# Earlier loads and earlier crossbar transposes in a windowed attention kernel with a gated feed-forward block

## The chip, the cores and the metric

One core of one Trainium2 chip. Times are device microseconds of whole executions; a profile's span is some 1.8 us shorter than the time of the same execution.

## The reference

Attention with a window of 128 and four sink tokens over 4 batches, 8 heads, 768 tokens and a head size of 64, then a gated feed-forward block on the 3072 tokens (512 to 1536 to 512):

```python
keep   = (pos_k < 4) | ((0 <= pos_q - pos_k) & (pos_q - pos_k < 128))
scores = np.where(keep, q @ k.T / 8, -1e9)
x      = softmax(scores) @ v                 # -> [3072, 512]
g      = x @ w_gate
out    = (g / (1 + np.exp(-g)) * (x @ w_val)) @ w_out
```

## The kernel before

Tokens go in twelve groups of 256. Scores of the first three groups read keys and queries transposed by TensorE; from group 3 on the sync queue transposes them on the way from SBUF to SBUF, through the crossbar, which is what `C(g)` does. The feed-forward work is a list of units, gate units and down units, over token tiles of 256, 256, 256, 512 and more. Attention steps hang on these units by number ("slots"), so that TensorE has matmuls to do meanwhile. VectorE works its own instructions in the order in which the program wrote them. A step may append work for VectorE to `later`; `flush()` at the end of a unit writes it out.

```python
def cross_T(g):
    t = crossp.tile([P, 2, 2, NP2, P], BF16, tag="kqT", name="kqT")
    for j in range(2):
        nc.sync.dma_start(t[:, j]..., nat[g][:, j]..., transpose=True)
    cross[g] = t

def step_ks(b):                    # sink keys and values of batch b
    ...
        nc.vector.tensor_copy(out=dst[r, :, h * NS:(h + 1) * NS],
            in_=... else cross[b * GC][r, 0, 0, :, 0:NS])
    nc.vector.tensor_tensor(vsb, vcf[...], diag_h[...], op=ALU.mult)

def gate(tb, f, attn):
    pg = project(wgs, "pg")        # TensorE into one PSUM bank
    th = ...                       # tanh on ScalarE
    for a in attn: a()             # the attention steps of this slot
    pv = project(wvs, "pv")
    # VectorE: u = (th + 1) * pg ; ht = u * pv
    flush()

def C(g):
    def last():
        cross_T(g)
        if g % GC == 0:            # groups 3, 6, 9: first of a batch
            later.append(A(step_ks, g // GC))
        next_load(g)
    return [last]
```

TensorE writes its products to PSUM, a memory of which this kernel takes a pool of eight banks, used in turn. When the turn comes round to a bank that VectorE has not read yet, TensorE stops.

The softmax here doesn't subtract the row's maximum and nothing guards it: scores larger than these inputs give would overflow.

## Time and profile before

| | before |
|---|---|
| time, median of 4 runs (lowest to highest) | 250.97 us (250.53 to 251.37) |
| span of the profiled run | 251.8 us |
| TensorE busy | 236.2 us |
| group 3's scores begin, after a wait of | 58.60 us, 1.58 us |
| VectorE waits for crossbar transposes | none |

The profiled run of this kernel took 253.56 us as timed. The lines of its profile are in the prediction. Two more matter for what came: the small sink copy of group 3 on VectorE, and the four crossbar transposes of groups 3 and 4 on the sync queue. In the timeline, a line is start, duration, engine, source line, operation and operands, and in brackets how long the engine was idle before it and for what.

```profile
46.32 12.80 SPq L285 DMA_TRANSPOSE kqT<-kq  x4
55.59 0.34 DVE L295 COPY ks<-kqT 64x16 bf16<-64x16 bf16 x2
```

The copy reads what the first of these transposes writes. It has no bracket: when VectorE came to it, the data were there.

### The profile page before, as it was taken

To read this page: it belongs to the slowest core of one execution; us is meant where nothing else is said; L and a number is where in the kernel's file an instruction comes from. 1 tells how busy PE (TensorE), PEld (TensorE's weight loads), DVE (VectorE), ACT (ScalarE), POOL (GpSimd) and SP (SyncE) were. 2 spreads that over 40 slices of the span, in tenths; PEclk is the share of its full clock that TensorE was granted. 3 is DMA by queue.
4 is the path that set the end of the run, shared out by engine and by line. 5 is a ranking of instruction groups with operands and counts; after the bars stand their busy time and mean duration, and the time that the engine had idled before them with its cause. 6 is when DMAs were issued, how large, how long until landed. Compare 5 with 4: busy or idle time off the path is not lost.

```text
span 251.8 us, 5130 instructions
## 1 busy us (share of the span) xinstructions
PE 236.2 (94%) x2043; PEld 133.8 (53%) x2043; DVE 161.7 (64%) x339; ACT 110.7 (44%) x219; POOL 67.6 (27%) x89
## 2 busy tenths in 40 slices
PE   7887889997999969999999999999999999999993
PEld 3456677885645424545345455445454445478441
DVE  3566878987753439995089894098991289887100
ACT  2646548336281346451283741374721562333121
POOL 4956446764595049203400000000000000000000
PEclk9999999999999979999999999999999999999999
DMA  6999999999999999936990162800263200200132
GB/s 160 127 192 186 205 189 196 158 124 146 128 179 202 230 170 136 96 44 141 177 185 0 22 108 65 205 24 1 41 86 104 107 0 0 44 0 0 53 116 85
DMA packets 102808, 27.90 MB, mean 111 GB/s; under 512 B 89984, under 2 KB 99712, under 8 KB 102784
## 3 DMA queue, kind: packets, MB, share of 16 engines
q0 software_dynamic: 71392, 13.64, 67.5%
q1 hardware_dynamic: 30816, 13.41, 25.1%
q10 hardware_dynamic: 576, 0.52, 0.8%
q8 instruction: 16, 0.26, 0.4%
q14 instruction: 8, 0.07, 0.1%
HBM read 28.34 MB, written 6.29 MB: 138 GB/s over the span
## 4 chain that ended last, share of the span: by engine, by line
PE 67%; DMA 20%; DVE 4%; POOL 4%; issue 2%; ACT 1%; SPq 1%; DVEq 0%; ACTq 0%
PE pd L462 25%; PE pv L434 18%; PE pg L434 16%; DMA kq<-in_q_dram 9%; DMA kqT<-kq 6%; DMA wg<-in_moe_w_gate_dram 4%; PE o L370 4%; PE s L323 3%; DVE u L447 1%; DMA st<-in_q_dram 1%; DVE ht L448 1%; DVE e L335 1%; POOL kq L96 1%; POOL va L123 1%; POOL kq L107 1%
## 5 line engine op out<-in xcount | busy, mean ns | idle before, releaser
L434 PE MATMUL pv<-xT,wv 128*128 128x256 bf16 (+1 forms) x384 | 75.1, 329 | 1.8 <-DMA wv<-in_moe_w_val_dram 1.1
L434 PE MATMUL pg<-xT,wg 128*128 128x256 bf16 (+1 forms) x384 | 74.6, 327 | 1.4 <-DMA wg<-in_moe_w_gate_dram 0.7
L441 ACT ACTIVATE th<-pg 128x512 f32<-128x512 f32 x72 | 43.4, 606 | 68.8 <-PE pg L434 68.3
L447 DVE SCALAR_TENSOR_TENSOR u<-th,pg 128x512 bf16<-128x512 f32 x72 | 49.2, 683 | 31.3 <-ACT th L441 30.9
L462 PE MATMUL pd<-wo,ht 128*128 128x512 bf16 x288 | 66.3, 379 | 0.0
L448 DVE TENSOR_TENSOR ht<-u,pv 128x512 bf16<-128x512 bf16 x72 | 49.5, 688 | 14.3 <-PE pv L434 7.3
L434 PEld LDWEIGHTS <-wg 128*128 128x128 bf16 x384 | 37.4, 98 | 28.3 <-issue 2.5
L330 ACT ACTIVATE e<-s 128x512 bf16<-128x512 f32 (+1 forms) x96 | 46.0, 582 | 6.2 <-PE s L323 6.1
L434 PEld LDWEIGHTS <-wv 128*128 128x128 bf16 x384 | 34.7, 98 | 22.4 <-issue 3.2
L462 PEld LDWEIGHTS <-ht 128*128 128x128 bf16 x288 | 26.8, 98 | 29.0 <-issue 0.3
L466 ACT ACTIVATE ot<-pd 128x512 f32<-128x512 f32 x24 | 14.5, 603 | 53.7 <-PE pd L462 53.7
L335 DVE TENSOR_TENSOR e<-e,mask 128x1024 bf16<-128x1024 bf16 (+1 forms) x48 | 29.3, 642 | 5.3 <-ACT e L330 5.2
L107 POOL DMA_DIRECT2D kq<-in_k_dram x18 | 16.0, 889 | 30.6 <-DMA kqT<-kq 26.8
L123 POOL DMA_DIRECT2D va<-in_v_dram x24 | 21.4, 901 | 10.1 <-DMA kq<-in_q_dram 3.8
L370 PEld LDWEIGHTS <-e 128*128 128x128 bf16 x352 | 16.6, 98 | 7.7 <-DVE e L335 1.9
L382 DVE TENSOR_TENSOR xn<-o,rcp 128x256 bf16<-128x256 f32 x46 | 19.5, 424 | 1.6
L370 PE MATMUL o<-va,e 128*128 128x65 bf16 x352 | 18.4, 193 | 1.2 <-DVE e L335 1.1
L107 POOL DMA_DIRECT2D kq<-in_q_dram x18 | 16.1, 892 | 3.0 <-DMA kq<-in_q_dram 1.5
L323 PE MATMUL s<-kqT 64*128 64x256 bf16 (+1 forms) x192 | 11.0, 243 | 3.5 <-DMA kqT<-kq 3.5
L375 DVE RECIPROCAL rcp<-o 128x4 f32<-128x4 f32 x48 | 8.3, 176 | 8.6 <-PE o L370 8.6
L323 PEld LDWEIGHTS <-kqT 64*128 64x128 bf16 x192 | 6.4, 96 | 10.1 <-issue 8.0
L370 PE MATMUL o<-vsb,es 128*128 128x260 bf16 x32 | 8.8, 275 | 0.4 <-ACT es L350 0.4
(55 smaller groups left out, 79.5 us busy)
## 6 DMA issues: line engine op xcount, KB each, us to landing
out_dram<-ot SPq DMA_DIRECT2D x24, 256.0 KB
va<-in_v_dram POOLq DMA_DIRECT2D x24, 128.0 KB, 8.6
kq<-in_k_dram POOLq DMA_DIRECT2D x18, 128.0 KB, 8.3
kq<-in_q_dram POOLq DMA_DIRECT2D x18, 128.0 KB, 8.1
wo<-in_moe_w_out_dram POOLq DMA_DIRECT2D x4, 384.0 KB, 12.4
wg<-in_moe_w_gate_dram POOLq DMA_DIRECT2D x4, 256.0 KB, 8.6
wv<-in_moe_w_val_dram POOLq DMA_DIRECT2D x4, 256.0 KB, 8.9
st<-in_q_dram ACTq DMA_DIRECT2D x4, 128.0 KB
```

The costliest lines, as they stand in the source:

```text
L107: nc.gpsimd.dma_start(x[:, j, i].rearrange("p (h d) -> p h d", d=D), src[b, :, t0:t0 + P].rearrange("h m d -> m h d"))
L123: nc.gpsimd.dma_start(va[:, j, :, 0:D], v[b, :, t0:t0 + P].rearrange("h m d -> m h d"))
L323: nc.tensor.matmul(pss[2 * pp + h][:, col:col + n * P], keys(b, t, r, p), queries(g, r, p, j, n), start=True, stop=True)
L330: nc.scalar.activation(e_t[g][:, h0 + h, lo:512], pss[2 * pp + h][:, lo:512], AF.Exp, scale=scale)
L335: nc.vector.tensor_tensor(e, e, m[:, :, lo:512].broadcast_to([P, 2, 512 - lo]), op=ALU.mult)
L370: nc.tensor.matmul(o, l, r, start=(i == 0), stop=(i == len(mms) - 1), skip_group_check=True)
L382: nc.vector.tensor_tensor(xns[g, j][:, 256 * hh:256 * (hh + 1)].rearrange("p (h d) -> p h d", h=4), po[:, :, 0:D], rcp.broadcast_to([P, 4, ...
L434: nc.tensor.matmul(ps[:, i * n:(i + 1) * n], ws[fi][:, c, fo * P:(fo + 1) * P], x[:, 0:n // P, c], start=(c == 0), stop=(c == DMC - 1))
L441: nc.scalar.activation(th, pg, AF.Tanh, scale=0.5)
L447: nc.vector.scalar_tensor_tensor(u, th, 1.0, pg, op0=ALU.add, op1=ALU.mult)
L448: nc.vector.tensor_tensor(hts[tb][:, f:f + two].rearrange("p a n -> p (a n)"), u, pv, op=ALU.mult)
L462: nc.tensor.matmul(po, hts[tb][:, f, ts * P:(ts + 1) * P], wos[f // n][:, f % n], start=(f == 0), stop=(f == DFC - 1))
```

## The change

The intent: bring data sooner (two larger loads per queue for the first group, GpSimd's loads no longer held back, the second group ahead of the second weight pair), and issue each crossbar transpose early, so that it only waits for its own data. The schedule of attention steps moves along, and one down unit goes in among the gate units.

```diff
-    for p in range(NP2):
-        st = opool.tile([P, 2, 4 * D], FP32, tag="ot", name="st")
+    for k2 in range(2):
+        st = natp.tile([P, 4, 4 * D], FP32, tag="kq", name="st")
...
-    give = const.tile([P, 1], FP32)
-    nc.gpsimd.tensor_copy(out=give, in_=first[0][:, 0, 0:1])
     load_v(0); load_gate(0)
+    load4(1)
     load_gate(1)
-    load4(1)
...  (first group: tile 1 is normalised first, on ScalarE)
-    us = [g0[0], g0[1], (alone, 0, 0), *g0[2:5], *g1, g0[5], *g2,
-          *downs(0), *downs(1), *downs(2)]
+    us = [g0[0], (alone, 0, 0), *g0[1:4], *g1, *g0[4:6], downs(0)[0], *g2,
+          downs(0)[1], *downs(1), *downs(2)]
...
-        (14, C(3)), ((16, 17), Ss(3)), (17, C(4)), ((18, 18, 19, 19), PVs(3)),
+        ... (10, K(2)), (10, C(3)), ... (13, C(4)),
+        ((16, 17), Ss(3)), ((18, 18, 19, 19), PVs(3)),
...
+        (22, C(5)), ((22, 22, 23, 23), PVs(4)), (24, Xs(4))))
     weave(gates(3) + downs(3), slots(
-        (0, C(5)), *pair(5, 6, 2), (3, C(6)), (12, C(7))))
+        *pair(5, 6, 2), (2, C(6)), (10, C(7))))
```

(One-line forms above are shortened from the source; slots of groups 1 and 2 are left out.)

More of the change, by code (lines that the diff above doesn't have):

```diff
@@ L167 @@
     first = []
-    for p in range(NP2):
-        st = opool.tile([P, 2, 4 * D], FP32, tag="ot", name="st")
+    for k2 in range(2):
+        st = natp.tile([P, 4, 4 * D], FP32, tag="kq", name="st")
         for i, src, eng in ((0, k, nc.sync), (1, q, nc.scalar)):
             eng.dma_start(st[64 * i:64 * (i + 1)],
-                          four_tokens(src, 0, slice(2 * p, 2 * p + 2)))
+                          four_tokens(src, 0, slice(4 * k2, 4 * k2 + 4)))
         first.append(st)
@@ L208 @@
     nc.vector.tensor_copy(out=flat0[:, 3 * P:4 * P], in_=flat[:, 3 * P:4 * P])
-    give = const.tile([P, 1], FP32)
-    nc.gpsimd.tensor_copy(out=give, in_=first[0][:, 0, 0:1])
     load_v(0)
     load_gate(0)
+    load4(1)
     load_gate(1)
-    load4(1)
-    load_gate(2)
     load_v(1)
-    load_gate(3)
-    load_gate(4)
+    for i in range(2, 5):
+        load_gate(i)
     kTs, qTs, es_t, e_t, xns, xTs = {}, {}, {}, {}, {}, {}
@@ L541 @@
     for ph in range(2):
-        transpose(0, ph, lambda p: first[p], id32)
+        transpose(0, ph, lambda p: first[ph][:, 2 * p - 4 * ph:2 * p - 4 * ph + 2], id32)
     step_S(0, 0)
@@ L546 @@
     warm(3)
+    pro(*[lambda: None] * 3)
+    step_PV(0, 1, 0, True)
+    step_PV(0, 0, 0)
+    later.insert(0, later.pop(1))
     flush()
-    for hh in range(2):
-        pro(A(step_PV, 0, 0, hh), A(step_PV, 0, 1, hh, True))
-        flush()
+    step_PV(0, 1, 1, True)
+    step_PV(0, 0, 1)
+    flush()
     warm(2)
@@ L565 @@
     g0, g1, g2 = gates(0), gates(1), gates(2)
-    us = [g0[0], g0[1], (alone, 0, 0), *g0[2:5], *g1, g0[5], *g2,
-          *downs(0), *downs(1), *downs(2)]
+    us = [g0[0], (alone, 0, 0), *g0[1:4], *g1, *g0[4:6], downs(0)[0], *g2,
+          downs(0)[1], *downs(1), *downs(2)]
     weave(us, slots(
-        (1, T(1)), (2, Ss(1) + [K(1)]), (4, PVs(1) + [flush]),
-        (5, [A(step_X, 1, 0), A(step_X, 1, 1, True), flush]),
-        (7, T(2)), ((8, 9), Ss(2)), (9, [K(2)]),
-        (10, PVs(2)[:2] + [flush]), (11, PVs(2)[2:] + [flush]),
-        (12, [A(step_X, 2, 0), A(step_X, 2, 1, True), flush]),
-        (14, C(3)), ((16, 17), Ss(3)), (17, C(4)), ((18, 18, 19, 19), PVs(3)),
+        (0, T(1)), (1, Ss(1) + [K(1)]), (3, PVs(1) + [flush]),
+        (4, [A(step_X, 1, 0), A(step_X, 1, 1, True), flush]),
+        (8, T(2)), ((9, 10), Ss(2)), (10, [K(2)]), (10, C(3)),
+        (11, PVs(2)[:2] + [flush]), (12, PVs(2)[2:] + [flush]),
+        (13, [A(step_X, 2, 0), A(step_X, 2, 1, True), flush]), (13, C(4)),
+        ((16, 17), Ss(3)), ((18, 18, 19, 19), PVs(3)),
         (20, Xs(3)), ((20, 21), Ss(4)), (21, [K(4)]),
-        ((22, 22, 23, 23), PVs(4)), (24, Xs(4))))
+        (22, C(5)), ((22, 22, 23, 23), PVs(4)), (24, Xs(4))))
     def pair(ga, gb, sh=0):
@@ L585 @@
     weave(gates(3) + downs(3), slots(
-        (0, C(5)),
-        *pair(5, 6, 2), (3, C(6)), (12, C(7))))
+        *pair(5, 6, 2), (2, C(6)), (10, C(7))))
     weave(gates(4) + downs(4), slots(*pair(7, 8), (3, C(8)), (10, C(9)), (14, C(10))))
```

## The prediction

> **What bounds the kernel now.** I read the page first, then the chain of work that ended last in order of time, then the waits of TensorE with its timeline, then the table of stretches around the two longest waits. The page says where the time can be.
>
> ```profile
> PE 236.2 (94%) x2043; PEld 133.8 (53%) x2043; DVE 161.7 (64%) x339; ACT 110.7 (44%) x219; POOL 67.6 (27%) x89
> PEclk9999999999999979999999999999999999999999
> DMA  6999999999999999936990162800263200200132
> ```
>
> TensorE is busy 236.2 of 251.8 us, so no schedule without less work gains more than 15.6 us, and part of that is the ends (1.43 us before the first matmul, some 3.5 us of last eviction and store). The DMA row is full for the first seventeen slices of 6.3 us: until about 107 us the loads are limited by supply. The clock row has one dip, in slice 15 (88.1 to 94.4 us). The chain shows which waits count:
>
> ```profile
> 0.81 3.07 DMA st<-in_q_dram
> 3.96 0.55 DMA vcf<-in_v_dram
> 5.07 1.93 POOL va L123 x2
> ...
> 11.28 10.82 DMA wg<-in_moe_w_gate_dram
> 22.38 0.69 POOL kq L96
> 23.21 12.56 DMA kq<-in_q_dram
> ...
> 38.32 9.81 DMA kq<-in_q_dram
> 48.19 10.28 DMA kqT<-kq
> 58.60 0.51 PE s L323 x8
> ...
> 84.43 0.60 ACT ot L466
> 85.49 1.28 SPq L285
> 86.87 3.90 DMA kqT<-kq
> 90.82 0.93 PE s L323 x10
> 91.75 1.82 PE pv L434 x4
> 93.57 1.25 PE pg L434 x4
> 94.82 0.86 PE pv L434 x4
> ```
>
> Up to 58.6 us the end is set by loads alone: from the wait of GpSimd for the first queries, through its queue of loads, to the queries of group 3 at 48.13 us, and 10.28 us of crossbar transposes behind those. TensorE has other waits before that (1.12 us for the second group's queries at 20.19, 0.23, 0.52 and 1.12 us for weights at 26.02, 29.95 and 32.58), but they are not on the chain: what they cost is given back at 58.6, where TensorE sits idle anyway. The second joint is at 84.43: the sync queue issues group 5's transposes only after the last store of the third token tile, whose eviction ends at 85.03. The timeline of TensorE has the waits themselves, and the table of stretches the clock behind the second:
>
> ```profile
> 58.60 0.51 PE L323 MATMUL s<-kqT 64*128 64x256 bf16 x8 [1.58 <-DMA kqT<-kq]
> 89.80 0.23 PE L323 MATMUL s<-kqT 64*128 64x128 bf16 x2 [1.14 <-DMA kqT<-kq]
> 90.82 0.93 PE L323 MATMUL s<-kqT 64*128 64x256 bf16 x10 [0.79 <-DMA kqT<-kq]
> 91.00:92.00 1.00, 1.00 (x11) 0.51 (x8) 0.00 (x0) 0.67 (x2) 0.38 (x1) 0.50 1.01 191
> ```
>
> The seventh figure after the stretch is the granted clock: 0.50. The clock record of the trace has it at half from 90.81 to 94.23 us. So the second wait costs twice: 1.14 + 0.79 = 1.93 us idle, and then the ten score matmuls take 0.93 us where the same kind takes about 0.45, the four "pv" 1.82 where the next four take 0.86, the four "pg" 1.25 against 0.86: 0.48 + 0.96 + 0.39 = 1.83 us more.
>
> **What the Trainium skill says.** "TensorE: Matmul & The Clock Gate", Part 1: TensorE's clock is gated to half after an idle window of about 3.4 us, and the windows run freely. The trace agrees on the length (3.41 us at half) and narrows the condition: the window before the drop, 87.40 to 90.81, was 1.93 us idle (56%), while the window 56.68 to 60.09 was 1.58 us idle (46%) and nothing dropped. "DMA: Bandwidth & Descriptors", Issuing engines are not separate DMA queues: transfers from the sync, scalar and GpSimd queues run on the same 16 engines and interleave. The trace agrees: between 48.2 and 58.6 us the transposes (0.60 MB) and the GpSimd loads (0.80 MB) share 136 GB/s. The same page, Specifications: below 512 B a transfer does not run at line rate. The trace agrees: loads that write 128-byte rows run at 154 GB/s (44 to 48 us), loads that write 512-byte rows at 192 (12 to 20 us), counted in what they write.
>
> **The change part by part.**
>
> First, the first keys and queries come by two loads of 256 KB per queue in place of four of 128 KB. The bytes are the same; the packets of these two queues flow without a gap from 2.3 to 6.5 us in the trace of before, so the engines set their pace, not the four issues of 0.65 us. Saved on the path: nothing. The second half may land a little later, because GpSimd's loads now run beside it.
>
> Second, the copy "give" goes, which held GpSimd from 2.53 until the first tile had landed (4.54), so that its loads began at 5.07. They can now begin at about 3.0 to 3.5 (a memset on VectorE at 3.22 comes before the first). In before, GpSimd's first bytes flow at 6.87, 1.8 us after its first issue; from 6.5 to 7.2 the engines are nearly empty (30 to 60 GB/s), and from 9 to 12 us they ramp at 100 to 154 GB/s to a steady 195. Had the engines no gap to fill, an earlier start would win nothing, as the work is conserved. The gap is worth about 0.6 us; the ramp of 3 us at some 130 in place of 195 is worth 1.0 us if a deeper queue removes it. The most is the shift of the issues itself, 1.5 to 2. I take 1.3 us for every load from there on, to the queries of group 3.
>
> Third, the second group's keys and queries go ahead of the second weight pair, and T(1) goes from the second gate unit to the first. This and the later place of the last weights (the units that need them come after the next four gates) should remove most of the 1.12 and 1.87 us of waits. Likewise the softmax of the first group, normalised for tile 1 first on ScalarE, should bring the first gate from 16.1 to about 15.4. All of this is hidden: it only brings TensorE sooner to group 3's scores.
>
> Fourth, at group 3's scores. C(3) and C(4) move ahead in the program, but the sync queue has nothing before them in either version except the small sink loads, and the first transpose waited for its data (46.32 and 48.13). So moving them changes nothing. The scores begin at 58.6 - 1.3 = 57.3. What does change is the work done by then: before, that point came after six units of g0, six of g1 and three and a half of g2; now it comes after one gate unit less (8 + 8 matmuls, 1.74 us) and one down projection more (12 x 0.216 = 2.6 us). So 0.86 us more is done. Stage gain: 1.3 + 0.86 = 2.2 us. TensorE would reach the point at about 55, so its wait grows from 1.58 to about 2 us, although the kernel is faster.
>
> Fifth, C(5) goes from the start of the third token tile to the second down unit of the second tile, ahead of two stores on the sync queue. Its loads were issued by 47.4 us, so the transposes can be done some 8 us before scores of group 5 are wanted at about 86. Gain: 1.93 us of waits, and 1.83 us of slow clock where that happens. In timed runs it may not: the profiled run took 253.56 us as timed, 2.3 us over the median, so the timed runs may have lacked the drop; on the other hand their spread is only 0.66 us, so it came in all of them or in none. I count it at 0.65: 1.2 us.
>
> Against it: the gate units after 57 us now carry all of PV(3), beside masks: VectorE has about 3.5 x 1.38 + 2.0 + 2.4 = 9.2 us of work in some 8 us of TensorE, so the transposes of group 3's output may wait some tenths: 0.4. And the longer wait at the scores may itself drop the clock in some runs: 0.2 x 1.7 = 0.3. C(6) and C(7), moved by one and two units, feed scores that do not wait: 0.
>
> Sum: 2.2 + 1.93 + 1.2 - 0.4 - 0.3 = 4.6 us, so 251.2 - 4.6 = **246.6 us**, 1.8% faster.
>
> **Rivals.** (a) The supply gains nothing: the engines' work is conserved, the first loads and GpSimd's merely swap, and group 3's queries land when they did. For it: the DMA row is full. Against it: the gap at 6.5 to 7.2. Then 0.86 + 1.93 + 1.2 - 0.7 = 3.3: 247.9. (b) The drop of the clock moves from 90.8 to the longer wait before 57.3 and is not removed. For it: that wait would be over half a window. Against it: it falls across a window's edge at 56.68 if the windows keep their place. Then the gain loses about 1.5 more than counted: 248.1. (c) The clock had dropped in all timed runs, and the ramp goes too (2 us of supply): 2.9 + 3.76 - 0.4 = 6.3: 245.0. (d) GpSimd's loads delay the first group so far that TensorE itself is late at group 3. It has about 2 us of slack there, and the second half of the first load would have to land at 9.5 or later in place of 7.7; unlikely. Then about 249.5.
>
> **Range and chances.** (a) and (b) set the upper end, (c) the lower: 244.8 to 248.7. The line of 2% is 246.2, close to the middle and a little under it: faster by over 2% 0.41, within 2% 0.57, slower by over 2% 0.02.
>
> **What would show it.** Right: GpSimd's first load at 3.0 to 3.5; no wait of TensorE for group 4's weights; group 3's scores at about 57.3 after a wait of about 2 us for the transposes; no wait for them at group 5's, and no half clock at 90. Wrong: scores of group 3 at 58.6 (the supply did not move), or a half clock just after them, or a wait at group 5's scores. If group 3's scores do not wait at all, the fourth step is wrong, as TensorE or VectorE then bounds that stage.

## The result

The changed kernel took 264.15 us (median of 4 runs, 261.7 to 265.07) against 250.97 us: slower by 5.1%, ratio 1.0511, 95% interval 1.0437 to 1.0585. I had said 246.6 us, with 2 chances in 100 of a slowdown by more than 2%. Ratios here and below are the mean time of one kernel's fast runs over that of the other's of the same rounds, so not quite the ratio of the medians. All outputs are right.

The page of the changed kernel, its busy row of TensorE and its clock by slice of 6.6 us:

```profile
PE 237.8 (91%) x2030; PEld 134.8 (51%) x2043; DVE 162.2 (62%) x339; ACT 110.7 (42%) x219; POOL 67.5 (26%) x88
PE   7789899439989996899999999999999999999994
PEclk9999999957999999799999999999999999999999
```

TensorE is busy about as long as before (237.8 us against 236.2). The time is in holes: slices 8 and 9, with reduced clock in slices 9 and 10, and a smaller one in slices 16 and 17. The chain of work that ended last, in order of time around the first hole:

```profile
45.30 8.51 DMA kqT<-kq
...
53.83 0.17 DVE ks L291
...
55.02 0.42 DVE xn L378
```

Before, the chain went from a transpose (48.19, 10.28 us) straight to the scores at 58.60. Now it goes from one to a copy of 0.17 us on VectorE. The timeline of the changed kernel shows both holes, and the sync queue:

```profile
45.30 11.90 SPq L281 DMA_TRANSPOSE kqT<-kq  x4
53.83 0.35 DVE L291 COPY ks<-kqT 64x16 bf16<-64x16 bf16 x2 [8.27 <-DMA kqT<-kq]
55.50 0.61 PE L458 MATMUL pd<-wo,ht 128*128 128x512 bf16 x1 [6.43 <-DVE xn L378]
104.44 0.35 DVE L291 COPY ks<-kqT 64x16 bf16<-64x16 bf16 x2 [3.46 <-DMA kqT<-kq]
106.16 1.63 PE L430 MATMUL pv<-xT,wv 128*128 128x512 bf16 x4 [3.74 <-DVE u L443]
```

The reader is to see three things. The first transposes were issued at 45.30 in place of 46.32, one microsecond sooner, as the loads came one microsecond sooner. VectorE came to the copy at 45.56, just after that issue, and stood there for 8.27 us, where the kernel before reached the same copy at 55.59 and did not wait. And TensorE stopped a few microseconds after VectorE, because a PSUM bank (that of the products "o", which "xn" reads) was not emptied. The profile puts TensorE's wait down to "xn", which is right and yet not the cause: the matmuls whose products the first "xn" reads ended at 45.39 us, and it stood in line behind the copy.

After the first hole the clock record has TensorE at half clock from 51.83 to 62.06 us, after the second from 106.44 to 109.85.

```profile
52.00:54.00 2.00, 0.00 (x0) 0.00 (x0) 0.17 (x1) 0.00 (x0) 0.37 (x2) 0.50 2.14 130
107.00:108.00 1.00, 1.00 (x3) 0.30 (x2) 0.67 (x2) 0.00 (x0) 1.00 (x2) 0.50 0.91 58
```

(The table of stretches: length, then busy time of TensorE, of its weight loads, VectorE, ScalarE and GpSimd, then the granted clock, the DMA share and GB/s.)

So my theory after the result: `C(3)` moves no transpose, but it carries `step_ks(1)` with it, and that moves a VectorE instruction ahead of its data. The rivals: the reordered units overload VectorE or the banks; or the transposes themselves have become late for whoever needs them first.

### The profile page after: what moved, and what is told of

Same layout as the page of the kernel before. It is cut to its first block, busy times and chain, and to the rows that moved or that the text cites.

```text
span 262.4 us, 5109 instructions
## 1 busy us (share of the span) xinstructions
PE 237.8 (91%) x2030; PEld 134.8 (51%) x2043; DVE 162.2 (62%) x339; ACT 110.7 (42%) x219; POOL 67.5 (26%) x88
## 4 chain that ended last, share of the span: by engine, by line
PE 63%; DMA 20%; DVE 10%; POOL 3%; issue 2%; ACT 1%; SPq 0%; DVEq 0%; ACTq 0%
PE pd L458 24%; PE pv L430 17%; PE pg L430 16%; DMA kq<-in_q_dram 9%; DMA kqT<-kq 7%; DMA wv<-in_moe_w_val_dram 4%; PE o L366 3%; DVE ht L444 2%; DVE u L443 2%; PE s L319 2%; DVE xn L378 2%; DVE e L331 2%; POOL kq L96 1%; POOL va L123 1%; PE px L402 1%
## 5 line engine op out<-in xcount | busy, mean ns | idle before, releaser
L458 PE MATMUL pd<-wo,ht 128*128 128x512 bf16 x276 | 67.4, 387 | 7.0 <-DVE xn L378 6.4
L366 PEld LDWEIGHTS <-e 128*128 128x128 bf16 x352 | 16.4, 98 | 7.2 <-DVE e L331 2.0
L319 PE MATMUL s<-kqT 64*128 64x256 bf16 (+1 forms) x192 | 10.4, 238 | 0.0
## 6 DMA issues: line engine op xcount, KB each, us to landing
wo<-in_moe_w_out_dram POOLq DMA_DIRECT2D x4, 384.0 KB, 12.4
```

The lines of the kernel that those rows point to most:

```text
L319: nc.tensor.matmul(pss[2 * pp + h][:, col:col + n * P], keys(b, t, r, p), queries(g, r, p, j, n), start=True, stop=True)
L366: nc.tensor.matmul(o, l, r, start=(i == 0), stop=(i == len(mms) - 1), skip_group_check=True)
L458: nc.tensor.matmul(po, hts[tb][:, f, ts * P:(ts + 1) * P], wos[f // n][:, f % n], start=(f == 0), stop=(f == DFC - 1))
```

## The experiments

Three calls, each with its own chip and its own runs of the kernel before (medians 250.86, 250.87 and 251.27 us).

### Both copies deferred, and each alone

```diff
-            if g % GC == 0:
+            if g % GC == 0 and g not in (3, 6):
                 later.append(A(step_ks, g // GC))
...
+        (19, [A(step_ks, 1)]), (20, Xs(3)), ...
...
-        *pair(5, 6, 2), (2, C(6)), (10, C(7))))
+        *pair(5, 6, 2), (2, C(6)), (10, C(7)), (11, [A(step_ks, 2)])))
```

> The changed kernel with one thing undone: the two small steps on VectorE that read the transposed keys (the sink copies ks of groups 3 and 6, with the product vsb after them) are emitted later, where the scores have already waited for these transposes; every load, transpose, matmul and its place stays. My theory (VectorE works its queue in program order and stands 8.3 and 3.4 us at these copies until the crossbar transposes land): both waits go, no half clock at 52 to 62 us, and the time falls from 264 to 245.5 to 248. Rival 1 (the down unit set between the gates overloads VectorE or the PSUM banks): VectorE still falls behind, the stall of 6.4 us before the first down unit stays for the most part, 258 to 264. Rival 2 (group 3's transposes themselves are late, and whatever needs them first stands): the stall moves to the scores of group 3, time 254 to 260.

Measured: 251.75 us (11 runs), ratio to before 1.0029 (1.0004 to 1.0053). Of the 13.2 us lost, 12.4 are back. Both waits of VectorE are gone, and the two rivals with them: the reordered units, the banks and the transposes are all still there. But the time is 3.75 us above the range that I expected. The timeline of TensorE shows where:

```profile
57.06 0.51 PE L319 MATMUL s<-kqT 64*128 64x256 bf16 x8 [0.32 <-DMA kqT<-kq]
67.98 0.28 PE L402 MATMUL px<-ident,xn 128*128 128x128 bf16 x2 [2.16 <-DVE xn L378]
```

Group 3's scores begin at 57.06, where the prediction had 57.3. Ten microseconds later the transposes of group 3's output wait 2.16 us for VectorE, which in that stretch has the gate units, the masks and now also my deferred copy with its product (1.04 us); behind the wait the clock record has half clock from 68.49 to 71.90.

> As e1, but only group 3's copy is deferred. My theory: the first stall (6.4 us before the down unit, about 3 us more around it, and most of 10.2 us at half clock) goes, the second (3.7 us before pv, and 3.4 us at half clock) stays: 250 to 253. If the second grows, because everything comes sooner while group 6's transposes do not, up to 254. Rivals 1 and 2 as for e1: 258 to 264.

Measured: 251.84 us (5 runs, 249.32 to 252.25), the same as with both deferred.

> As e1, but only group 6's copy is deferred. My theory: the stall of 3.7 us before pv and the half clock after it (about 1.7 us) go, the first stall stays: 257.5 to 260. If the two were one cause that feeds on the first, the time would stay at 262 to 265 or fall as far as e1.

Measured: 259.35 us (4 runs), ratio 1.0355 (1.0323 to 1.0387). So deferring group 6's copy alone takes off 4.8 us, but beside the other deferral it takes off nothing. The second hole thus feeds on the first, and not only adds to it: C(6) with its copy in place costs nothing that the runs can tell once the first hole is gone. The traces show how. With group 3's copy deferred, the timeline has group 6's transposes, the next loads and the copy at

```profile
87.08 3.15 SPq L281 DMA_TRANSPOSE kqT<-kq  x2
89.38 0.88 POOL L107 DMA_DIRECT2D kq<-in_k_dram  x1 [11.36 <-DMA kqT<-kq]
93.61 0.34 DVE L291 COPY ks<-kqT 64x16 bf16<-64x16 bf16 x2
```

and in the changed kernel at

```profile
90.19 0.88 POOL L107 DMA_DIRECT2D kq<-in_k_dram  x1 [12.65 <-DMA kqT<-kq]
94.36 5.76 SPq L281 DMA_TRANSPOSE kqT<-kq  x2
```

Group 5's transposes free the buffer that GpSimd's loads of group 9 wait for. Without the first hole, group 6's transposes are issued 2.3 us ahead of these loads, and all their packets have passed by 92 us. In the changed kernel they come 4.2 us behind the loads, share the DMA engines with them and take until 104.4: ten microseconds. VectorE comes to the copy at 100.98 and stands there for the last 3.46 us of them.

### One part of the change alone, in the kernel before

```diff
-        (14, C(3)), ((16, 17), Ss(3)), (17, C(4)), ...
+        (9, C(3)), ((16, 17), Ss(3)), (17, C(4)), ...
```

> The kernel before with one part of the change alone: the unit of group 3's transposes goes from slot 14 to slot 9 (with the copy that hangs on it). My theory: the sync queue issues the transposes no sooner (about 46.3 us, when the loads have landed), but VectorE stands at the copy from about 43 to 54 us and TensorE behind it; 256 to 262. Rival 1 (the fault is in the reordered gate and down units): 250.5 to 252, nothing changes.

Measured: 260.55 us (4 runs), ratio 1.0399 (1.0374 to 1.0424). Nothing else is changed here, so this one move costs 9.7 us. In its timeline:

```profile
46.24 12.01 SPq L285 DMA_TRANSPOSE kqT<-kq  x4
54.99 0.35 DVE L295 COPY ks<-kqT 64x16 bf16<-64x16 bf16 x2 [10.15 <-DMA kqT<-kq]
56.66 0.61 PE L434 MATMUL pg<-xT,wg 128*128 128x256 bf16 x2 [8.32 <-DVE xn L382]
```

The transposes are issued at 46.24 in place of 46.32: moving them five units ahead moved them by 0.08 us, less than two traces of the same order differ (45.88 in the next run). The next run takes this apart once more, with the transposes at slot 9 and only the copy left behind:

```diff
+        (9, C(3)), (14, [lambda: later.append(A(step_ks, 1))]), ((16, 17), Ss(3)), ...
```

(with the condition of the first experiment for group 3)

> The kernel before with group 3's transposes at slot 9, as in the run that was 9.7 us slower, but the copy on VectorE left at slot 14. My theory: the place of the transposes themselves is without effect, as the sync queue has nothing else to do: 250.3 to 251.5, no wait of VectorE for the transposes. Rival: the earlier issue itself hurts (the sync queue or the next loads that hang on it): 255 to 261.

Measured: 251.18 us (20 runs, one of them slow at 253.48; 251.13 without it), ratio 1.0013 (0.9991 to 1.0035). In its timeline the copy does not wait:

```profile
45.88 11.99 SPq L285 DMA_TRANSPOSE kqT<-kq  x4
54.82 0.34 DVE L295 COPY ks<-kqT 64x16 bf16<-64x16 bf16 x2
```

`C(3)` also calls `next_load`, which writes loads for GpSimd and a memset for VectorE; these moved along in both runs. So the place of the transposes and of these loads has no effect that the runs can tell, and the 9.4 us between the two runs are the place of the copy (with the product `vsb` behind it) alone.

```diff
-        ((22, 22, 23, 23), PVs(4)), ...        (0, C(5)),
+        (22, C(5)), ((22, 22, 23, 23), PVs(4)), ...
```

> The kernel before with group 5's transposes alone moved from the first gate of the third tile to the second down unit of the second, ahead of two stores. If the wait at group 5's scores costs what I predicted, the time falls by 1.9 us (248.5 to 249.5), by up to 3.8 in runs that had the half clock. If it frees buffers for loads that then run beside group 6's transposes, VectorE may stand at group 6's copy instead: 250.5 to 253.

Measured: 249.3 us (20 runs), ratio 0.9948 (0.9928 to 0.9968). The part of the change that does move a transpose ahead of other work of its queue is worth 1.3 to 1.6 us (by the ratio and by the medians). The waits at group 5's scores are gone. VectorE stands 0.21 us at group 6's copy, so the danger that I had named is near, but not reached.

### What is left of the gain

The first experiment had lost its gain to a wait for VectorE at group 3's output. Here the copy and those transposes go later:

```diff
-        (19, [A(step_ks, 1)]), (20, Xs(3)), ((20, 21), Ss(4)), ...
+        (20, [A(step_ks, 1)]), (21, Xs(3)), ((20, 21), Ss(4)), ...
```

> The changed kernel with both copies deferred, as in the run of 251.75 us, and two more moves: the copy of group 3 goes behind the PSUM transposes' unit, and the transposes of group 3's output go one down unit later, so that VectorE has caught up. My theory: there the gain of 3.9 us by group 5's scores was lost to a wait of 2.16 us for xn and 1.7 us of half clock behind it; without these 247 to 248.8. Rival: the loss is elsewhere (the later gates are limited by VectorE in any case) and the wait only moves: 250.5 to 252.

Measured: 247.83 us (6 runs), ratio 0.9876 (0.9841 to 0.9911). It is as expected: neither the wait nor the half clock is there, and the time is 1.2 us from my prediction for the whole change. It was run again in the third call:

> The run of 247.83 us again, for a comparison on the same chip: 247.4 to 248.4.

Measured: 247.96 us (6 runs), ratio 0.9865 (0.9841 to 0.9890).

The next run gives it the old start (four loads of 128 KB per queue, and the copy "give"):

> As the run before it in this call, but with the old start: four loads of 128 KB per queue and the copy that holds GpSimd back. My theory: the new start brings group 3's data about 1 us sooner, so this is 0.6 to 1.3 us slower than its neighbour, with the scores of group 3 at about 58 us. Rival: the early start of GpSimd's loads delays the first keys as much as it wins later, or the scores do not wait: within 0.3 us.

Measured: 249.06 us (16 runs), ratio to before 0.9927 (0.9901 to 0.9952); so 1.2 us slower than its neighbour by the medians. The timelines of TensorE, new start and then old:

```profile
56.95 0.51 PE L319 MATMUL s<-kqT 64*128 64x256 bf16 x8 [0.69 <-DMA kqT<-kq]
```

```profile
57.93 0.51 PE L321 MATMUL s<-kqT 64*128 64x256 bf16 x8 [2.15 <-DMA kqT<-kq]
```

The scores come 0.98 us later, after a longer wait, although TensorE reached its first gate sooner (15.38 us against 16.44). Behind the wait of 2.15 us this profile has half clock from 59.02 to 62.43. By its 16 runs, the nine with a mean clock of 0.997 or more took 248.49 us (median) and the seven below it 249.99. This suggests that such a wait costs 1.5 us more where the clock falls; where it fell in the runs without a profile is not known. Compared with the nine alone, the new start is worth 0.7 us.

The new start has two parts. With GpSimd still set free but the first loads small again:

> As the run of 247.83 us, but the first keys and queries by four loads of 128 KB per queue as in the kernel before; the copy that held GpSimd back stays away. It separates the two parts of the new start. My theory: the early loads of GpSimd bring group 3's data sooner, and the size of the first loads only moves the first group: its second half lands at 7.7 to 8.2 in place of 8.4 to 8.9 us, the first gate starts some 0.5 us sooner, and the time stays within 0.5 us of 247.8. Rival: the larger loads are what brings the data sooner: 248.5 to 249.

Measured: 248.42 us (4 runs), ratio 0.9894 (0.9858 to 0.9930), 0.46 us above its neighbour (247.96), with overlapping intervals. By the letter of what I expected it lies between my theory (up to 248.3) and the rival (from 248.5), so the time does not decide. The trace speaks against the rival: group 3's scores begin at 56.50 us, no later than with large loads (56.79). The reason inside my theory was wrong: the first gate came at 16.37, not half a microsecond sooner than with large loads (16.43), and the second half landed at 8.81 in place of 8.40. So a gain or loss by the larger loads is not shown, and what delays the first group, by about 1 us against the old start (15.38), is GpSimd's early loads beside it.

Last, the remaining wait at group 3's scores, covered by one more gate unit:

```diff
-        ((16, 17), Ss(3)), ((18, 18, 19, 19), PVs(3)),
+        ((17, 18), Ss(3)), ((19, 19, 20, 20), PVs(3)),
```

> As the run of 247.83 us, but the scores and products of group 3 one unit later, so that the last wait for the crossbar (0.69 us) is covered by a gate unit. If that wait is still on the path: 246.9 to 247.5. If the later products make group 3's output late again on VectorE: 247.8 to 249.5.

Measured: 247.29 us (6 runs), ratio 0.9848 (0.9817 to 0.9879), the best version here: 1.5% faster than the kernel before and 6% faster than the changed one. Against the 247.96 the step of 0.7 us is about the wait that went, but the two intervals overlap, so the step alone is not shown.

## Why the prediction was wrong

**The step that failed** is the fourth: "C(3) and C(4) move ahead in the program, but the sync queue has nothing before them in either version except the small sink loads, and the first transpose waited for its data (46.32 and 48.13). So moving them changes nothing." The half about the sync queue was right, and the run with the transposes moved and the copy left shows it (251.18 us). The conclusion was wrong, because I asked only what the queue of the moved instruction does, not what else the moved step writes into other queues. `C(3)` also appends the copy for VectorE, and VectorE works in order. The Trainium skill has this in "TensorE: Matmul & The Clock Gate", in the table at the head of the page: the queues of ScalarE, VectorE and GpSimd are strict FIFO. The trace agrees: nothing ran on VectorE from 45.56 to 53.83 us, though the matmuls that the four evictions "xn" behind the copy wait for had all ended by 48.20 us. The same mistake stands once more in the line on C(6) and C(7), "moved by one and two units, feed scores that do not wait: 0". C(6) has such a copy too, and VectorE stood 3.46 us at it, though only behind the first hole.

What it cost, an estimate from the changed kernel's own profile: 6.43 us idle before the down unit and 1.24 us at the transposes behind it; half clock until 62.06, some 2.6 us (half of the 5.1 us of matmuls from 55.50 on); 3.74 us idle at the second hole and 1.7 us of half clock behind it. That is 15.7 us; less the gain of 3 us that the later versions show, it is 12.7 of the 13.2 us measured.

**The supply**: I took 1.3 us. GpSimd began at 2.49 us, sooner than the 3.0 to 3.5 I had written, as its first load did not wait for the memset; the transposes were issued 1.02 us sooner, and group 3's scores came 0.98 us sooner than with the old start. Single traces scatter: over all thirteen the first transpose is issued at 45.51 to 46.45 with the old start (five traces) and at 44.80 to 45.30 with GpSimd set free (eight). The mechanism was right and the size nearly so. Group 3's scores at 57.06 and 56.95, with the copies deferred, answer to the 57.3 predicted.

**TensorE's slack there**: I expected a wait of about 2 us. It was 0.32 and 0.69 us. The first gate came at 16.4 to 16.9 us (17.6 in one trace) in place of 15.4, since GpSimd's loads delayed the first group's second half to 8.4 to 8.9 us; I had named that, but put no size to it.

**Group 5's transposes**: 1.93 us of waits and 1.2 us for the clock predicted, 1.3 to 1.6 us measured alone. The half clock of the profiled run was counted at 0.65; that run was slower than any other of the kernel, so this was probably too much. How often the clock falls there in ordinary runs is not settled: their mean clock alone does not show it (43 of the 79 runs at 0.997 or more, with a median only 0.17 us lower).

**VectorE behind group 3's scores**: 0.4 us predicted, 1.21 us of wait in the changed kernel. In the first experiment it was 2.16 us and half clock, of which my own placing of the copy is part. Moved out of the way, it gave 3.9 us (251.75 to 247.83).

With the failed step mended and that backlog out of the way, the kernel is at 247.3 to 248.0 us, where the sum of the other steps was 246.6. The missing 0.7 to 1.4 us could be what group 5's transposes gave less than predicted (1.5 to 1.8 us), but that is not shown.

## What to carry to other kernels

When a step moves in the program, list what it writes into every engine's queue, and for each of these ask when its data come; a transfer that waits early in an otherwise empty queue was harmless here, while a copy of 0.17 us that waits in VectorE's queue stops all that stands behind it, and through the PSUM banks TensorE too. Keep the consumer apart from the issue of its transfer: issue early, once you have looked at what the issue sets free for other queues, and write the consumer where something else has already waited for the same data. A wait that a profile puts down to an engine's instruction may belong to the instruction ahead of that one in the same queue.

## What the Trainium skill lacked or had wrong

- "TensorE: Matmul & The Clock Gate", Part 1: it ties the half clock to an idle window of about 3.4 us, and does not say how idle. In the trace before, a window 56% idle (1.93 us of 3.41) was enough and one 46% idle was not; in all thirteen traces the sixteen windows before a drop were 56% idle or more, and the idlest of the others at full clock was 52% idle. After the stall of 6.43 us the clock stayed at half for 10.24 us, three windows of 3.41: the first all idle, the second 50% idle, the third full of matmuls.
- "DMA: Bandwidth & Descriptors", Latency and other measured facts: it gives a bandwidth of 261 GB/s for crossbar transposes. Beside GpSimd's loads one transpose of 128 by 1024 bf16 (262 KB) took 8.51 us from issue to landing, with the next two issued behind it in that time (47.11 and 50.74), and two took 10.1 us (94.36 to 104.4), which makes 52 GB/s. The page has no figure for that case, and a schedule has to reckon with it.
- No page that I read says that a small instruction written ahead of its transfer can stop TensorE by way of the PSUM banks; here it cost 9.4 us of 250 by itself.
